# A tile per row for x, seven quarter products one chunk earlier, and a spread attention plan

## The chip, the cores and the metric

The kernel runs on one core of one Trainium2 chip. A core has five engines that run side by side, each through its own queue in order: TensorE (PE in the profile; its weight loads are PEld), VectorE (DVE), ScalarE (ACT), GpSimd (POOL) and SyncE (SP, which here only issues DMAs). Engines wait for each other through semaphores. Matmul results land in PSUM, eight banks of 512 fp32 columns on 128 partitions; the other engines carry them from there into SBUF. The metric is the device time of one execution in microseconds (us), the median over several runs.

## What is computed

Eight batch rows of causal attention with 8 heads, 576 positions and 64 features a head; four heads see a window of 32 positions, four a window of 128 with every fourth position. The rows' outputs, written one behind another as 4608 tokens of 512 features, go through a feed-forward layer with a squared ReLU:

```python
scores = scale * np.matmul(q, k.transpose(0, 1, 3, 2))        # (8, 8, 576, 576)
mask_plain = (rel >= 0) & (rel < 32)                            # heads 0..3
mask_dil = (rel >= 0) & (rel < 128) & (rel % 4 == 0)            # heads 4..7
attn = softmax(np.where(masks, scores, -1e9))
x = np.matmul(attn, v).transpose(0, 2, 1, 3).reshape(4608, 512)
r = np.maximum(x @ w_in, 0.0)                                   # w_in 512 x 2048
out = (r * r) @ w_out                                           # w_out 2048 x 512
```

## The kernel before

**Chunks and rows.** The tokens are cut into nine chunks of 512 (chunk 0 takes the 576 of row 0, chunk 1 only 448), and attention works by rows of 576. x, transposed, lies in one ring tile `xT` for three rows (lines 88 and 89); token t is column t mod 1728. Chunk c needs the end of one row and the start of the next. While TensorE multiplies chunk c, the attention of row c+1 is put between its matmuls.

**First product** (`mm1_gen`, L260 in `mm1_tile`): 16 slices of 128 hidden features, each 4 matmuls over the 512 inputs, into one of four PSUM banks used in turn. ScalarE does the ReLU into `rt` (L269), VectorE squares two slices at a time into `g` (L294). A slice gives two steps (`yield`), so a first product is 32 steps. A chunk that lies across the ring's end (chunks 3 and 6) is multiplied in two pieces, each with its own weight load.

**Second product.** Chunks 0 to 3 use `mm2_by_rows_gen` or `mm2_gen`: 64 matmuls of 512 columns (L301), 32 steps. Chunks 4 to 8 use `seven_gen`: quarter blocks of `g` and `w_out` and their sums, seven products of 16 matmuls of 256 columns each (L396), 28 steps. The sums of `g` (`S1`, `S2`, `S3`, lines 376 to 382) are made by VectorE behind the squares: `sums_behind` adds one behind the squares of steps 20 and 24, two behind those of 28 and 32. The sums of `w_out` (`T1` to `T4`, L365, eight subtractions) are made once, in chunk 2, every seventh step from step 4 on. VectorE also adds the seven products up (lines 450 to 491).

**Attention parts** (`row_parts`). s0, s1 (plain heads) and z0, z1 (dilated heads) make scores: matmuls into two PSUM pairs (L588, L602), two exps on ScalarE (L569), one product with the mask on VectorE (L573). They write `AT`, of which there is one. a0 to a2, d0, d1, e0, e1 multiply with v into one pair (L641, L655); VectorE normalizes them into `x_p` or `x_d` (L626, L627). x0, x1 and y0, y1 transpose the result into one pair (L670, L688), and ScalarE copies that into `xT` (L676, L694); x0 needs a0 and a1, x1 needs a1 and a2, y0 needs d0 and d1, y1 needs e0 and e1. From chunk 0's second product on the pairs are only two, used in turn, so each part waits for the one or two before it to be emptied. For rows 2 and 3 the transposes use a bank of the matmuls in place of a pair.

**The order** is written out by hand: a plan is a string of `step:part`, `run` sorts the parts by step and lets the matmul generator go on to each part's step before it. Each engine's queue follows from that order.

**Loading a row.** GpSimd issues the DMAs of q and k (L147, L223) and copies the plain heads into token order (`in_token_order`, L230); SyncE issues the transposing DMAs of the dilated heads (L248), stores of that copy (L236) and its transposing DMAs (L244), and the loads of v; GpSimd casts v (L202, L206). This goes one row ahead. For row 2 it stands in front of chunk 0's second product, whose plan is

```python
"4:t0 6:t1 8:s0:u0 10:s1:u1 12:z0 14:z1 18:a0 19:a1 20:a2 21:x0 22:d0 23:x1"
" 24:d1 25:e0 26:e1 27:y0 28:y1"
```

Of the kernel before, what the change touches and what calls it, by code (L numbers as in the profile page):

```python
# [8 lines left out]
FP16 = mybir.dt.float16  # L9
# [4 lines left out]
P = 128  # L14
# [3 lines left out]
def kernel(  # L18
# [9 lines left out]
    nc = tc.nc  # L28

    B, H, S, D = q.shape  # L30
    W = 32
    DIL = 4
# [4 lines left out]
    NDM = DM // P  # L37
# [18 lines left out]
    const = ctx.enter_context(tc.tile_pool(name="const", bufs=1))  # L56
# [18 lines left out]
    def bank(dt=FP32):  # L75
        i = turn["bank"] % 4
        turn["bank"] += 1
        b = PS[:, i, :]
        return b if dt == FP32 else b.bitcast(dt)
# [5 lines left out]
        return b if dt == FP32 else b.bitcast(dt)  # L85


    RING = 3 * S
    xT = const.tile([P, NDM, RING], FP16, name="xT")


    WI = ((0, 512), (512, 1024), (1024, 2048))
# [10 lines left out]
    def w_in_of(dmk, ffc):  # L103
        f = 512 * (ffc // 4) + ffc % 4
        t = 0 if f < 512 else 1 if f < 1024 else 2
        f -= WI[t][0]
        return wi[t][:, dmk, f : f + 509 : 4]
# [86 lines left out]
    def copy(eng, o, i):  # L194
        if eng is nc.scalar:
            nc.scalar.copy(o, i)
        else:
            eng.tensor_copy(o, i)
# [26 lines left out]
            )  # L225
        return d

    def in_token_order(b, n):
        o = natp.tile([P, 9, HH, D], FP16, name=f"o{b}", tag="o")
        nc.gpsimd.tensor_copy(o, n.rearrange("p h j d -> p j h d"))  # L230
        return o

    def keep_sliding_qk(b, o):
        d = dpool.tile([2, S, HH * D], FP16, name=f"dp{b}", tag="dp")
        for i in (1, 0):
            nc.sync.dma_start(  # L236
                out=d[i].rearrange("(p j) x -> p (j x)", j=9),
                in_=o[64 * i : 64 * (i + 1)].rearrange("p j h d -> p (j h d)"),
            )
        return d  # L240

    def transpose_sliding(b, dp):
        for i in (1, 0):
            nc.sync.dma_start_transpose(out=QKTp[b % 2][:, i, :, PADP:], in_=dp[i])  # L244

    def transpose_dilated(b, dd):
        for i in (1, 0):
            nc.sync.dma_start_transpose(out=QKTd[b % 2][:, i, :, KPAD:], in_=dd[i])  # L248
# [3 lines left out]
    def mm1_tile(ffc, t0, t1, rt):  # L252
        w = t1 - t0
        ph = bank()
        o = t0 % RING
        cut = min(w, RING - o)
        for dmk in range(NDM):
            for a, b, x in ((0, cut, o), (cut, w, 0)):
                if a < b:
                    nc.tensor.matmul(  # L260
                        ph[:, a:b],
                        w_in_of(dmk, ffc),
                        xT[:, dmk, x : x + b - a],
                        start=(dmk == 0 and a == 0),
                        stop=(dmk == NDM - 1 and b == w),
                    )
            if dmk == 1:
                yield
        nc.scalar.activation(rt, ph[:, 0:w], ACTF.Relu)  # L269
# [51 lines left out]
    def mm2_gen(c):  # L321
        for t in range(TOKC // P):
            po = bank()
            for ffc in range(NFF):
                mm2(c, po, t, ffc)
                if ffc % 2 == 1 and ffc < NFF - 1:
                    yield
            store(c, t, po)
            yield
# [165 lines left out]
    def moe_gen(c):  # L495
        yield from mm1_gen(c)
        yield from mm2_gen(c)

    def moe_seven_gen(c):
        yield from mm1_gen(c, sums_behind)  # L500
        yield from seven_gen(c)
# [162 lines left out]
    def x_sliding(b, half, xs, wide):  # L664
        px = pt(wide)
        for m3 in range(3):
            m = 3 * half + m3
            x = xs[m // 2][:, m % 2].rearrange("p h d -> p (h d)")
            for c in range(2):
                nc.tensor.transpose(  # L670
                    px[:, 288 * c + QB * m3 : 288 * c + QB * (m3 + 1)],
                    x[:, P * c : P * (c + 1)],
                    ident[0:QB, 0:QB],
                )
        t0 = (b % 3) * S + 288 * half
        nc.scalar.copy(  # L676
            xT[:, 0:2, t0 : t0 + 288],
            px[:, 0:UW].rearrange("x (c t) -> x c t", c=2),
        )

    def x_dilated(b, t, xs, wide):
        py = pt(wide)
        for a in range(2):
            for e in range(2):
                x = xs[a][:, e].rearrange("p h d -> p (h d)")
                for c in range(2):
                    o = 288 * c + QD * (2 * a + e)
                    nc.tensor.transpose(  # L688
                        py[:, o : o + QD],
                        x[0:QD, P * c : P * (c + 1)],  # L690
                        ident[0:QD, 0:QD],
                    )
        t0 = (b % 3) * S + 288 * t
        nc.scalar.copy(  # L694
            xT[:, 2:4, t0 : t0 + 288].rearrange("x c (i r) -> x c i r", r=DIL),
            py[:, 0:UW].rearrange("x (c r i) -> x c i r", c=2, r=DIL),
        )

    def row_parts(b, wide):

        xs, ys, zs = [], [], []
        return {
            "s0": lambda: s_sliding(b, 0),
            "s1": lambda: s_sliding(b, 1),
            "z0": lambda: s_dilated(b, 0),
            "z1": lambda: s_dilated(b, 1),
            "a0": lambda: xs.append(av_sliding(b, 0)),
            "a1": lambda: xs.append(av_sliding(b, 1)),
            "a2": lambda: xs.append(av_sliding(b, 2)),
            "x0": lambda: x_sliding(b, 0, xs, wide),  # L710
            "x1": lambda: x_sliding(b, 1, xs, wide),
            "d0": lambda: ys.append(av_dilated(b, 0, 0)),
            "d1": lambda: ys.append(av_dilated(b, 0, 1)),
            "e0": lambda: zs.append(av_dilated(b, 1, 0)),
            "e1": lambda: zs.append(av_dilated(b, 1, 1)),
            "y0": lambda: x_dilated(b, 0, ys, wide),
            "y1": lambda: x_dilated(b, 1, zs, wide),
        }

    def run(*plans, more=()):  # L720


        todo = list(more)
        for plan, parts in plans:
            for w in plan.split():
                step, *names = w.split(":")
                todo += [(int(step), parts[n]) for n in names]
        at = 0
        for step, part in sorted(todo, key=lambda t: t[0]):
            pump(step - at)  # L730
            at = max(at, step)
            part()
        pump(1000)
# [162 lines left out]
    n, dd = load_whole_sliding_qk(2), keep_dilated_qk(2)  # L896
    cast_sliding_v(1, 2)
    for t in range(2):
        for a in range(2):
            cast_dilated_v(1, t, a)  # L900
    o = in_token_order(2, n)
    transpose_dilated(2, dd)
    transpose_sliding(2, keep_sliding_qk(2, o))
    pending.append(mm2_by_rows_gen(0))
    parts = row_parts(1, True)
    parts.update(
        t0=lambda: t_sliding(1, ns1, 0),
        t1=lambda: t_sliding(1, ns1, 1),
# [5 lines left out]
            "4:t0 6:t1 8:s0:u0 10:s1:u1 12:z0 14:z1 18:a0 19:a1 20:a2 21:x0 22:d0 23:x1"  # L914
            " 24:d1 25:e0 26:e1 27:y0 28:y1",
            parts,
        )
    )
    load_v(2)

    rows_ = {b: row_parts(b, b > 3) for b in range(2, B)}
    SCORES = "{}:s0 {}:s1 {}:z0 {}:z1"
    VALUES = "{}:a0 {}:a1 {}:a2 {}:x0 {}:d0 {}:x1 {}:d1 {}:e0 {}:e1 {}:y0 {}:y1"
    for c in range(1, NTOKC):
        b = c + 1
        if b + 1 < B:
            see(QKTp[b % 2][0:1, 0, 0, PADP : PADP + 1])  # L930
            n, dd = load_whole_sliding_qk(b + 1), keep_dilated_qk(b + 1)
            o = in_token_order(b + 1, n)
            transpose_dilated(b + 1, dd)
            transpose_sliding(b + 1, keep_sliding_qk(b + 1, o))
        if b < B:
            cast_v(b)
        if b + 1 < B:
            load_v(b + 1)
        pending.append(moe_gen(c) if c < 4 else moe_seven_gen(c))
        plans, more = [], []  # L940
        if c < 3:
            plans.append((SCORES.format(*range(24, 40, 4)), rows_[b]))
            plans.append((VALUES.format(*range(40, 62, 2)), rows_[b]))
        if c == 2:
            it = sum_w_out_gen()
            more = [(4 + 7 * i, lambda it=it: next(it)) for i in range(8)]
        if c == 3:
            plans.append((SCORES.format(2, 8, 14, 20), rows_[b]))
            plans.append((VALUES.format(*range(24, 46, 2)), rows_[b]))
            plans.append((SCORES.format(47, 51, 55, 59), rows_[b + 1]))  # L950
        if 3 < c < B - 1:
            plans.append((VALUES.format(2, 5, 8, 11, 13, 16, 18, 22, 26, 29, 32), rows_[b]))
        if 3 < c < B - 2:
            plans.append((SCORES.format(36, 42, 48, 54), rows_[b + 1]))
        run(*plans, more=more)


# [28 lines left out]
```

## Time and profile before

| | |
|---|---|
| median of 3 runs | 311.64 us (311.43, 311.64, 315.43) |
| the profiled execution | 313.25 us, its span 311.2 us |
| granted TensorE clock | 1.00 throughout |
| matmul starts at chunk 0 | 20.0 us |
| DMA | 46.73 MB, mean 150 GB/s |
| L260, first product | 768 matmuls |
| L301, second product whole | 256 matmuls |
| L396, second product in seven | 560 matmuls |

The span runs from the first to the last instruction; the rest of the execution's time lies around it. A row of the timeline gives start, duration, engine, line, operation, what is written from what, the shape, how many instructions are merged, and in brackets the idle time before and what ended it. A matmul's duration holds the way through the array, so the distance between two starts is what it takes from the queue. The rows by stage give, for a window in us, the length of the window, then busy time and instructions of PE, PEld, DVE, ACT and POOL, the granted clock, the mean number for the DMA share, and GB/s.

By the starts of its first products the chunks begin at: c1 65.4, c2 96.1, c3 128.5, c4 163.3, c5 194.7, c6 226.3, c7 255.4, c8 281.4 us.

### The profile page before, as it was taken

The numbers are of one execution on the slowest core, as the hardware profiler recorded it, in microseconds if no ns is written. First come the engines' busy times: TensorE is split into PE (matmuls) and PEld (weight loads), VectorE is DVE, ScalarE is ACT, GpSimd is POOL, SyncE is SP. The second block draws the span as 40 slices with busy tenths as digits, with TensorE's granted clock in tenths as the row PEclk, the third lists the DMA queues.
The fourth block names the chain that finished last, engine by engine and source line by source line (L and its number), as shares of the span: only waits on it lengthen the run. The fifth ranks groups of instructions, "written<-read, shape, count | busy, mean of one in ns | idle before, by whom it ended". The sixth has DMA issues, their size and how long they took to land.

```text
span 311.2 us, 7133 instructions
## 1 busy us (share of the span) xinstructions
PE 297.2 (95%) x2932; PEld 200.7 (65%) x2932; DVE 198.2 (64%) x354; ACT 161.8 (52%) x286; POOL 85.4 (27%) x120
## 2 busy tenths in 40 slices
PE   3988999899999999999999999999999999999995
PEld 3657954455555555687545578657888885685584
DVE  6545645835852986297345879686868753863674
ACT  2646857278536772686356653565456406504610
POOL 5591027132703913283350344006000000000000
PEclk9999999999999999999999999999999999999999
DMA  7999989699979999998938894886120020012012
GB/s 117 242 205 212 213 185 234 156 227 206 224 180 220 266 196 164 248 235 166 236 134 185 162 216 122 190 173 141 67 71 3 2 101 34 2 46 91 0 36 101
DMA packets 75376, 46.73 MB, mean 150 GB/s; under 512 B 54416, under 2 KB 71056, under 8 KB 75152
## 3 DMA queue, kind: packets, MB, share of 16 engines
q1 hardware_dynamic: 67952, 32.52, 44.4%
q0 software_dynamic: 7248, 13.63, 24.7%
q8 instruction: 23, 0.38, 0.5%
q10 hardware_dynamic: 144, 0.13, 0.1%
q14 instruction: 9, 0.07, 0.1%
HBM read 39.85 MB, written 16.52 MB: 181 GB/s over the span
## 4 chain that ended last, share of the span: by engine, by line
PE 92%; DVE 2%; DMA 2%; ACT 2%; issue 1%; POOL 0%; DVEq 0%; POOLq 0%
PE PS L260 41%; PE PS L396 20%; PE PS L301 17%; PE PS L655 3%; PE PS L588 2%; PE PS L641 2%; PE PS L602 2%; DMA nd<-in_q_dram 2%; PE PS L688 1%; PE PS L670 1%; PE PS L523 1%; DVE AT L573 1%; ACT AT L569 1%; PE PS L581 1%; DVE x_p L627 1%
## 5 line engine op out<-in xcount | busy, mean ns | idle before, releaser
L260 PE MATMUL PS<-xT,wi 128*128 128x512 f16 (+6 forms) x768 | 136.1, 329 | 2.9 <-ACT xT L676 1.7
L269 ACT ACTIVATE rt<-PS 128x512 f16<-128x512 f32 (+2 forms) x160 | 88.7, 555 | 66.8 <-PE PS L260 64.0
L260 PEld LDWEIGHTS <-wi 128*128 128x128 f16 x768 | 79.2, 114 | 42.1 <-issue 3.0
L294 DVE TENSOR_TENSOR g<-rt 128x1024 f16<-128x1024 f16 (+1 forms) x64 | 47.6, 747 | 38.5 <-ACT rt L269 38.4
L301 PE MATMUL PS<-wo,g 128*128 128x512 f16 x256 | 64.4, 379 | 0.0
L569 ACT ACTIVATE AT<-PS 128x576 f16<-128x576 f32 x64 | 38.4, 650 | 19.8 <-PE PS L602 12.1
L396 PEld LDWEIGHTS <-S 128*128 128x128 f16 x320 | 31.0, 98 | 3.8
L301 PEld LDWEIGHTS <-g 128*128 128x128 f16 x256 | 21.3, 97 | 18.2
L396 PE MATMUL PS<-T,S 128*128 128x256 f16 x240 | 28.2, 273 | 0.0
L573 DVE TENSOR_TENSOR AT<-AT,maskp 128x1152 f16<-128x1152 f16 x14 | 15.0, 1072 | 19.1 <-ACT AT L569 19.1
L202 POOL CAST vp<-sv 128x512 f16<-128x512 f32 x24 | 20.6, 874 | 23.6 <-DMA sv<-in_v_dram 23.6
L206 POOL CAST vd<-sd 128x512 f16<-128x512 f32 x32 | 23.7, 773 | 10.5 <-DMA sd<-in_v_dram 10.4
L396 PEld LDWEIGHTS <-g 128*128 128x128 f16 x240 | 23.0, 98 | 3.2
L627 DVE TENSOR_TENSOR x_d<-PS,rcp_d 72x512 f16<-72x512 f32 x32 | 22.0, 687 | 1.1
L230 POOL COPY o<-n 128x2304 f16<-128x2304 f16 x6 | 13.0, 2172 | 30.6 <-issue 29.4
L396 PE MATMUL PS<-wo,g 128*128 128x256 f16 x160 | 19.5, 273 | 0.0
L676 ACT COPY xT<-PS 128x576 f16<-128x576 f16 x16 | 10.2, 637 | 14.6 <-PE PS L670 14.5
L573 DVE TENSOR_TENSOR AT<-AT,maskd 128x1152 f16<-128x1152 f16 x14 | 12.8, 917 | 7.3 <-ACT AT L569 7.3
L627 DVE TENSOR_TENSOR x_p<-PS,rcp_p 96x512 f16<-96x512 f32 x24 | 16.5, 687 | 0.8
L655 PEld LDWEIGHTS <-AT 128*128 128x128 f16 x256 | 12.4, 102 | 7.0 <-DVE x_d L627 1.3
L311 ACT COPY ot<-PS 128x512 f32<-128x512 f32 x16 | 9.4, 587 | 14.4 <-PE PS L301 14.4
L283 DVE TENSOR_TENSOR g<-rt 128x288 f16<-128x288 f16 x32 | 9.9, 309 | 9.9 <-ACT rt L269 9.8
(86 smaller groups left out, 257.3 us busy)
## 6 DMA issues: line engine op xcount, KB each, us to landing
sv<-in_v_dram SPq DMA_DIRECT2D x40, 128.0 KB, 4.0
out_dram<-c SPq DMA_DIRECT2D x19, 256.0 KB, 2.5
sd<-in_v_dram SPq DMA_DIRECT2D x8, 512.0 KB, 12.2
out_dram<-ot SPq DMA_DIRECT2D x15, 256.0 KB, 12.2
dp<-o SPq DMA_DIRECT2D x12, 288.0 KB, 3.8
sd<-in_v_dram SPq DMA_DIRECT2D x8, 288.0 KB
wo<-in_moe_w_out_dram POOLq DMA_DIRECT2D x4, 512.0 KB, 13.7
n<-in_k_dram POOLq DMA_DIRECT2D x6, 288.0 KB, 5.8
```

What stands on the lines that cost most here:

```text
L202: nc.gpsimd.tensor_copy(vp[b % 2][:, m : m + 2, :, 0:D], sv[:, m : m + 2, :, :])
L206: nc.gpsimd.tensor_copy(vd[b % 2][:, t, c : c + 2, :, 0:D], sd[:, t, :, D * c : D * (c + 2)].rearrange("p h (c d) -> p c h d", d=D),)
L230: nc.gpsimd.tensor_copy(o, n.rearrange("p h j d -> p j h d"))
L260: nc.tensor.matmul(ph[:, a:b], w_in_of(dmk, ffc), xT[:, dmk, x : x + b - a], start=(dmk == 0 and a == 0), stop=(dmk == NDM - 1 and b == w),)
L269: nc.scalar.activation(rt, ph[:, 0:w], ACTF.Relu)
L294: nc.vector.tensor_mul(g[:, f2 : f2 + 2, o:TOKC], rt[:, :, o:TOKC], rt[:, :, o:TOKC])
L301: nc.tensor.matmul(po, g[:, ffc, o + t * P : o + (t + 1) * P], w_out_of(ffc), start=(ffc == 0), stop=(ffc == NFF - 1),)
L396: nc.tensor.matmul(po[t], lhs(j)[:, t * P : (t + 1) * P], rhs(j), start=j == 0, stop=j == HF - 1)
L569: nc.scalar.activation(AT[:, u + i, 0:UW], ps[:, :, 0 : UW // 2], ACTF.Exp, scale=scale)
L573: nc.vector.tensor_mul(AT[:, u : u + n, 0:UW], AT[:, u : u + n, 0:UW], mask.unsqueeze(1).to_broadcast([P, n, UW]),)
L627: nc.vector.tensor_tensor(out=x[0:w], in0=pv[:, :, :, 0:D], in1=rcp[0:w].unsqueeze(3).to_broadcast([w, 2, HH, D]), op=ALU.mult,)
L655: nc.tensor.matmul(pav[:, e, h * (D + 2) : h * (D + 2) + D + 1], AT[:, 4 + 2 * a + t, off : off + P], vd[b % 2][:, t, 2 * a + e, h, 0 : D ...
```

## The change

x gets one tile a row in place of the ring, so every chunk that holds parts of two rows (2 to 7) is multiplied in two pieces. Chunk 3 uses the seven quarter products, and the sums of `w_out` are made at steps 4, 7, ... 25 of chunk 2. Plans are now a table by chunk: row 4's parts are spread over the whole of chunk 3, and of the next row's four score parts chunk 3 holds one, chunk 4 two and chunk 5 all four, where all three held all four; what is left over comes early in the following chunk. Row 2's copy into token order moves from GpSimd to ScalarE, and it and the DMAs that follow it are issued at step 17 of chunk 0's second product.

```diff
-    RING = 3 * S
-    xT = const.tile([P, NDM, RING], FP16, name="xT")
+    xT = [const.tile([P, NDM, S], FP16, name=f"xT{r}") for r in range(3)]
...
-    def in_token_order(b, n):
+    def in_token_order(b, n, eng=nc.gpsimd):
         o = natp.tile([P, 9, HH, D], FP16, name=f"o{b}", tag="o")
-        nc.gpsimd.tensor_copy(o, n.rearrange("p h j d -> p j h d"))
+        copy(eng, o, n.rearrange("p h j d -> p j h d"))
         return o
...
-        o = t0 % RING
-        cut = min(w, RING - o)
+        rows_in = [(r, max(t0, r * S), min(t1, (r + 1) * S)) for r in range(t0 // S, (t1 - 1) // S + 1)]
         for dmk in range(NDM):
-            for a, b, x in ((0, cut, o), (cut, w, 0)):
-                if a < b:
-                    nc.tensor.matmul(
-                        ph[:, a:b],
-                        w_in_of(dmk, ffc),
-                        xT[:, dmk, x : x + b - a],
-                        start=(dmk == 0 and a == 0),
-                        stop=(dmk == NDM - 1 and b == w),
-                    )
+            for r, a, b in rows_in:
+                nc.tensor.matmul(
+                    ph[:, a - t0 : b - t0],
+                    w_in_of(dmk, ffc),
+                    xT[r % 3][:, dmk, a - r * S : b - r * S],
+                    start=(dmk == 0 and a == t0),
+                    stop=(dmk == NDM - 1 and b == t1),
+                )
...
-    o = in_token_order(2, n)
-    transpose_dilated(2, dd)
-    transpose_sliding(2, keep_sliding_qk(2, o))
+
+    def turn_row_2():
+        transpose_dilated(2, dd)
+        transpose_sliding(2, keep_sliding_qk(2, in_token_order(2, n, nc.scalar)))
+
...
-        )
+        ),
+        more=[(17, turn_row_2)],
     )
     load_v(2)
...
+    SEVEN = 3
+    rows_ = {b: row_parts(b, b > SEVEN) for b in range(2, B)}
     SCORES = "{}:s0 {}:s1 {}:z0 {}:z1"
     VALUES = "{}:a0 {}:a1 {}:a2 {}:x0 {}:d0 {}:x1 {}:d1 {}:e0 {}:e1 {}:y0 {}:y1"
+    FAR = SCORES.format(*range(24, 40, 4)) + " " + VALUES.format(*range(40, 62, 2))
+    PLANS = {
+        1: (FAR, ""),
+        2: (FAR, ""),
+        3: (
+            SCORES.format(2, 8, 14, 20)
+            + " "
+            + VALUES.format(24, 27, 30, 33, 35, 38, 40, 44, 48, 51, 54),
+            "57:s0",
+        ),
+        4: (
+            "2:s1 7:z0 13:z1 " + VALUES.format(10, 15, 18, 21, 24, 27, 29, 33, 37, 40, 43),
+            "47:s0 53:s1",
+        ),
+        5: (
+            "2:z0 8:z1 " + VALUES.format(4, 7, 10, 13, 16, 18, 20, 24, 28, 31, 34),
+            SCORES.format(38, 43, 48, 53),
+        ),
+        6: (VALUES.format(2, 5, 8, 11, 13, 16, 18, 22, 26, 29, 32), ""),
+    }
...
-        pending.append(moe_gen(c) if c < 4 else moe_seven_gen(c))
-        plans, more = [], []
-        if c < 3:
-            plans.append((SCORES.format(*range(24, 40, 4)), rows_[b]))
-            plans.append((VALUES.format(*range(40, 62, 2)), rows_[b]))
-        if c == 2:
+        pending.append(moe_gen(c) if c < SEVEN else moe_seven_gen(c))
+        more = []
+        if c == SEVEN - 1:
             it = sum_w_out_gen()
-            more = [(4 + 7 * i, lambda it=it: next(it)) for i in range(8)]
-        if c == 3:
-            plans.append((SCORES.format(2, 8, 14, 20), rows_[b]))
-            plans.append((VALUES.format(*range(24, 46, 2)), rows_[b]))
-            plans.append((SCORES.format(47, 51, 55, 59), rows_[b + 1]))
-        if 3 < c < B - 1:
-            plans.append((VALUES.format(2, 5, 8, 11, 13, 16, 18, 22, 26, 29, 32), rows_[b]))
-        if 3 < c < B - 2:
-            plans.append((SCORES.format(36, 42, 48, 54), rows_[b + 1]))
-        run(*plans, more=more)
+            more = [(4 + 3 * i, lambda it=it: next(it)) for i in range(8)]
+        now, ahead = PLANS.get(c, ("", ""))
+        run((now, rows_.get(b)), (ahead, rows_.get(b + 1)), more=more)
```

In the copies L676 and L694 the target becomes `xT[b % 3]` with columns counted from the row's start.

More of the change, by code (lines that the diff above doesn't have):

```diff
@@ L674, in x_sliding @@
                 )
-        t0 = (b % 3) * S + 288 * half
+        t0 = 288 * half
         nc.scalar.copy(
-            xT[:, 0:2, t0 : t0 + 288],
+            xT[b % 3][:, 0:2, t0 : t0 + 288],
             px[:, 0:UW].rearrange("x (c t) -> x c t", c=2),
@@ L692, in x_dilated @@
                     )
-        t0 = (b % 3) * S + 288 * t
+        t0 = 288 * t
         nc.scalar.copy(
-            xT[:, 2:4, t0 : t0 + 288].rearrange("x c (i r) -> x c i r", r=DIL),
+            xT[b % 3][:, 2:4, t0 : t0 + 288].rearrange("x c (i r) -> x c i r", r=DIL),
             py[:, 0:UW].rearrange("x (c r i) -> x c i r", c=2, r=DIL),
@@ L916 @@
             parts,
-        )
+        ),
+        more=[(17, turn_row_2)],
     )
     load_v(2)
-    rows_ = {b: row_parts(b, b > 3) for b in range(2, B)}
+    SEVEN = 3
+    rows_ = {b: row_parts(b, b > SEVEN) for b in range(2, B)}
     SCORES = "{}:s0 {}:s1 {}:z0 {}:z1"
     VALUES = "{}:a0 {}:a1 {}:a2 {}:x0 {}:d0 {}:x1 {}:d1 {}:e0 {}:e1 {}:y0 {}:y1"
+    FAR = SCORES.format(*range(24, 40, 4)) + " " + VALUES.format(*range(40, 62, 2))
[18 more added lines that the diff above has]
+    }
     for c in range(1, NTOKC):
```

## The prediction

> **What bounds the kernel.** I read the page's busy shares and its chain first.
>
> ```profile
> PE 297.2 (95%) x2932; PEld 200.7 (65%) x2932; DVE 198.2 (64%) x354; ACT 161.8 (52%) x286; POOL 85.4 (27%) x120
> PE 92%; DVE 2%; DMA 2%; ACT 2%; issue 1%; POOL 0%; DVEq 0%; POOLq 0%
> ```
>
> TensorE is the bound. A part is worth what it takes from TensorE's queue, or from a wait in front of it. Next the sums by stage; c0 to c8 are the chunks.
>
> ```profile
> 146.00:163.42 17.42, 17.42 (x168) 8.59 (x166) 7.57 (x13) 8.59 (x15) 8.57 (x11) 1.00 0.76 184
> ...
> 180.74:194.85 14.11, 14.11 (x169) 11.79 (x168) 11.48 (x15) 6.16 (x11) 6.93 (x8) 1.00 0.71 163
> ...
> 243.31:255.54 12.23, 12.23 (x113) 10.93 (x112) 7.83 (x12) 1.48 (x3) 0.00 (x0) 1.00 0.13 46
> 255.54:269.35 13.81, 13.81 (x66) 7.29 (x65) 7.11 (x11) 8.96 (x15) 0.00 (x0) 1.00 0.11 37
> ```
>
> The first row is c3's second product (64 matmuls of 512 columns, plus attention), the second c4's with seven quarter products and four score parts, the third c6's with the seven alone, the last c7's first product: 64 matmuls of 512 columns, 0.2158 us each. So a step of the plans (two such matmuls) is 0.432 us, and a score part is (14.11 - 12.23) / 4 = 0.47.
>
> Then the waits on TensorE. From 66 us on, starts are a matmul's own time apart but for two waits of size. The timelines of c4 and c5 show them:
>
> ```profile
> 178.34 0.38 PE L260 MATMUL PS<-xT,wi 128*128 128x512 f16 x1
> 178.55 0.64 ACT L694 COPY xT<-PS 128x576 f16<-128x576 f16 x1
> ...
> 179.24 1.24 PE L260 MATMUL PS<-xT,wi 128*128 128x512 f16 x5 [0.51 <-ACT xT L694]
> ```
>
> ```profile
> 209.51 0.42 PE L688 MATMUL PS<-ident,x_d 72*128 72x72 f16 x8
> 210.66 0.59 PE L260 MATMUL PS<-xT,wi 128*128 128x512 f16 x2 [0.73 <-ACT xT L694]
> ```
>
> c4 multiplies rows 3 and 4 while that copy writes row 5's columns; c5 the like. They share only the one ring tile.
>
> In c0 a different wait, in its timeline:
>
> ```profile
> 53.62 2.11 POOL L230 COPY o<-n 128x2304 f16<-128x2304 f16 x1 [1.22 <-DMA n<-in_q_dram]
> ...
> 54.07 2.27 DVE L573 TENSOR_TENSOR AT<-AT,maskd 128x1152 f16<-128x1152 f16 x1 [0.94 <-ACT AT L569]
> ...
> 57.23 0.43 PE L641 MATMUL PS<-vp,AT 128*128 128x65 f16 x8 [1.09 <-DVE x_p L627]
> ```
>
> Beside GpSimd's copy the mask product takes 2.27 us; alone (52.36) it takes 0.76. The first x_p stands behind it, and the third value part waits for the PSUM pair that x_p empties.
>
> Last, the cost of short pieces, in c6, and of VectorE's sums, in c4:
>
> ```profile
> 227.20 0.42 PE L641 MATMUL PS<-vp,AT 128*128 128x65 f16 x8
> 227.46 1.47 PE L260 MATMUL PS<-xT,wi 128*128 128x384 f16 x12
> 228.77 0.42 PE L641 MATMUL PS<-vp,AT 128*128 128x65 f16 x8
> ```
>
> ```profile
> 178.60 0.68 DVE L294 TENSOR_TENSOR g<-rt 128x1024 f16<-128x1024 f16 x1
> 179.20 0.68 DVE L378 TENSOR_TENSOR S<-g 128x1024 f16<-128x1024 f16 x1
> 179.92 0.69 DVE L380 TENSOR_TENSOR S<-S,g 128x1024 f16<-128x1024 f16 x1
> ```
>
> Six pairs of 384 + 128 take 1.31 us, 0.2183 a pair: cutting costs 2.5 ns. Eight 65-column matmuls, each with its own weights, go every 0.0325 us (0.26 a part). A square and two sums hold VectorE for 2.0 us.
>
> **The change, part by part** (us of TensorE's time).
>
> *Seven products in c3:* 12.23 for 13.81, -1.58.
>
> *A tile per row:* in c4 the next matmul starts 0.90 after the one before, 0.68 late; in c5 209.51 + 0.26 = 209.77, so 0.89 late. A copy to another tile can hold no matmul: -1.57.
>
> *The price of the tiles:* today c3 and c6 are cut (at the ring's end); then every chunk from c2 to c7. c2, c4 and c5: 64 x 2.5 ns = 0.16 each, +0.48. c7 is cut 448 + 64, and no row has 64 columns on these weights. Between the pace of 65 columns (0.0325) and that of c6's 128-column piece (0.2183 - 0.1625 = 0.056) the pair is 0.1891 + 0.0325 to + 0.056, against 0.2158: +0.36 to +1.9. I take 0.36, since 65 columns is nearest. The same columns stream, so no gain is possible.
>
> The Trainium skill ("TensorE: Matmul & The Clock Gate", section "LDWEIGHTS (loading the stationary operand)") gives a load as its column count over 1.2 GHz, 107 ns for 128. By that rule, as an estimate, no piece could be shorter than 107 ns: the new cuts would cost about 10 us (3.4 in c2, 0.2 in c4, 1.7 in c5, 5.2 in c7) and the change would lose. c6 speaks against it: its 128-column pieces start the next matmul 56 ns later, weights included.
>
> *Row 2's copy on ScalarE.* ScalarE's relus take 543 ns for 448 columns and 598 for 512, 0.86 ns a column; from the 638 ns of a 576-column copy that makes 2.1 us for 2304. It stands behind the last exp (done 54.04; n landed by 53.62), so it runs until 56.2. Behind it in ScalarE's queue stand row 1's copies into xT, the first today at 58.51, at 57.3 then: 1 us to spare. At half the pace it would cost 1. On SyncE the moved transposes and stores pass nothing: chunk 0's output stores come from step 26 on, and o is wanted at 58.01, behind the dilated transposes. On GpSimd nothing follows until 66.7. VectorE's mask is then done at 54.8, the first x at 55.96 (value part 54.60 to 54.86, 0.17 to VectorE, 0.24 + 0.69); the third value part starts at 56.0 instead of 57.23: -1.2. The parts after it keep their distances.
>
> *w_out's sums every third step:* eight subtractions now at steps 4 to 25 of c2, where GpSimd's copy and casts (100.68 to 110.2) make VectorE's squares 1.09 long. By the queue the last square ends about 114.0 and the second product wants it at 113.9: +0.1 (0 to 1; nothing waited there before, so no gain).
>
> *The spread plans.* Score and value parts stay the same in number; their places change what stands in VectorE's queue. A part waits for a PSUM pair, and two pairs alternate; a value part's pair is free when VectorE has normalized it. c3 loses its waits of 0.15 and 0.16 in front of parts at 143.30 and 147.99: -0.3. New waits, walked through the queues with the durations above:
>
> - c5: z0 at step 2, a0 at 4, a1 at 7, z1 at 8. From c5's start: z0 0.86 to 1.33; ScalarE: relu 1.03, exps 1.54 and 2.09, done 2.74; a0 2.24 to 2.50; VectorE: mask 2.77, square 3.44, a0's reciprocal 4.04, its x done 4.97; a1 3.80 to 4.06, its x done 5.81. z1 would run at 4.49 and 4.72 and needs both pairs: its second half starts at 5.85, 1.1 late. Later e1 (28) stands behind a square and two sums, so y1 (34) comes 0.5 late. +1.6.
> - c4: a0's x (step 10) stands behind z0's mask and a square and is done 7.37 us into the chunk; z1 (13) wants the pair at 7.1: 0.3. d0's x (24) stands behind a square and a sum, done 16.1; d1 (29) wants its pair at 15.9: 0.2. e0's x (33) stands behind the last square and two sums, done 22.1; y0 (40) wants it at 21.7: 0.4. +0.9.
> - c3: its first product now has the sums too. By the clock of before: square 6 runs at 144.6, two sums until 146.6, a2's x (30) until 147.5; d0 (35) wants the pair at 146.7: +0.9.
>
> Each is 0 if the queue drains faster than this walk. Transposes landed for row 5 at 144.8 and row 6 at 175.8; their scores come later than that in both versions, so DMA stays hidden; were it not, every late microsecond would count whole.
>
> *Sum:* -1.58 - 1.57 - 1.2 - 0.3 = -4.65; +0.48 + 0.36 + 0.1 + 0.9 + 0.9 + 1.6 = +4.34. Net -0.3. The profiled run took 313.25 (span 311.2, 2.05 around it), 1.6 above the median of 311.64. The difference applied to the median gives 311.3.
>
> **Rivals.**
>
> *No new waits* (for: c4 and c5 of before run seven products, sums and values and waited for no pair; against: there value parts came before the sums of their step, and no score part came between). -4.65 + 0.94 = -3.7: 307.9.
>
> *GpSimd's copy lands on c4's sums: slower.* Row 7's copy starts 20 us after c3's end today (183.36 after 163.25). The new plan has c4's last sums at about 19.7 to 21.2. If the copy starts before the last sum has, VectorE is held 2 us as in c0, e0's pair with it, and y0 waits 2 longer: 313.3; with c5 slowed by the casts for row 7 (0.9) 314.2. Against: c3's last store, which row 6's transposes follow, comes later.
>
> *The ring is not the cause:* the two waits go on in c5, or show up as another wait on the copy: +0.9 to +1.6, 312.2 to 312.9. Against: c6, the same plan, does not wait, so it depends on columns.
>
> **How the numbers follow.** Forecast 0.5 (alone 309.8 to 312.6); no waits 0.22; copy on the sums 0.2; ring not the cause 0.08. The range takes in all four: 308.0 to 314.2. 2% (6.2 us, about what a measurement here tells from no change) lies outside all: even without any cost the gains stop at 4.65. Faster 0.03, within 0.93, slower 0.04.
>
> **What would show it.** c3's second product with no 512-column matmuls; no wait of L260 on L694 after 66 us; pieces of 128, 256, 320 columns in c2, c4, c5, and c7's first product 0.3 longer; no 2.27 us mask in c0 and the third value part 1.2 us earlier; in c5 z1's second half (L602) waiting about 1 us for x_p. If c5 shows no such wait, the walk is wrong and the time is near 308. If c7's first product grows by over 1 us, the 64-column price was wrong.

## The result, and the profile after

The changed kernel takes 314.44 us in the median of 20 runs (313.41 to 318.93), the kernel before 312.25 beside it (20 runs, 311.43 to 315.43). The ratio of the runs is 1.006, its 95% interval 1.0039 to 1.008: slower by about 1.9 us (the medians alone are 2.2 us apart), where 0.3 us less was forecast. The time lies just above the range; 0.6 of the 3.1 us between forecast and median is the kernel before, whose median is 312.25 over these runs and was 311.64 over three.

The profiled execution after took 313.48 us (span 311.5, before 311.2). Its page, engines and chain of waits:

```profile
PE 295.4 (95%) x3236; PEld 222.0 (71%) x3236; DVE 204.9 (66%) x369; ACT 162.2 (52%) x284; POOL 83.3 (27%) x119
...
PE 81%; DVE 8%; DMA 5%; ACT 2%; POOL 1%; issue 1%; POOLq 0%; ACTq 0%
```

TensorE is as busy as before, with 304 more and shorter matmuls. The chain is the news: VectorE's part of it went from 2% to 8%, which points to waits for VectorE. The windows by stage say where. Columns as before: window, its length, busy time and instructions of PE, PEld, DVE, ACT, POOL, clock, DMA share, GB/s; the rows are c3's second product, c4's second, c5's first and second, and c7's first:

```profile
143.79:159.54 15.75, 15.11 (x187) 13.04 (x185) 12.79 (x25) 4.93 (x8) 8.35 (x11) 1.00 0.82 190
177.43:192.01 14.58, 14.35 (x170) 12.37 (x168) 13.06 (x20) 4.84 (x8) 7.45 (x8) 1.00 0.67 163
192.01:210.91 18.90, 18.04 (x238) 15.62 (x237) 13.47 (x25) 12.54 (x22) 1.55 (x3) 1.00 0.86 186
210.91:226.29 15.38, 14.54 (x179) 12.09 (x178) 12.09 (x18) 6.89 (x12) 4.64 (x5) 1.00 0.20 62
255.34:269.54 14.20, 14.20 (x130) 9.39 (x128) 6.99 (x11) 8.96 (x15) 0.00 (x0) 1.00 0.11 38
```

In c5 TensorE is idle for 0.86 and 0.84 of these lengths; in c7 for nothing, there the short pieces themselves cost. Set out by the distance from the first matmul of a chunk to that of the next (us, worked out from the starts in the two traces):

| chunk | before | after | difference | predicted difference |
|---|---|---|---|---|
| c0, c1 | 76.09 | 74.57 | -1.52 | -1.2 |
| c2 | 32.37 | 32.61 | +0.24 | +0.26 |
| c3 | 34.79 | 32.42 | -2.37 | -2.39 |
| c4 | 31.43 | 32.48 | +1.05 | +0.85 |
| c5 | 31.64 | 34.27 | +2.63 | +1.81 |
| c6, c8 | 54.97 | 54.97 | 0 | 0 |
| c7 | 26.04 | 26.44 | +0.40 | +0.36 |

(The predicted differences are the terms of the sum put to their chunks, with 0.47 for each score part that the plans move: three out of c3, one into c4, two into c5.) From c2 on the changed kernel is 1.95 us longer, which is what the runs measure. The profile alone would have said otherwise: in its c0 and c1 this execution is 1.5 us ahead, and that is not there in the mean over executions, as the experiments show. Of the 1.52, 0.97 lies in c0's second product. The other 0.55 lies in its first, where the matmuls of 288 columns start every 0.222 us at first and every 0.123 us later: until 24.6 us in the profile before, until 21.8 in the one after. The profile after gives a granted clock of 0.50 for 19.4 to 22.7 us; the one before gives 1.00 there at the same slow pace, so "1.00 throughout" in the table of before does not describe its start.

In c0 the copy is now on ScalarE, and the second mask beside it takes 0.76:

```profile
53.51 2.11 ACT L195 COPY o<-n 128x2304 f16<-128x2304 f16 x1
53.65 0.76 DVE L570 TENSOR_TENSOR AT<-AT,maskd 128x1152 f16<-128x1152 f16 x1 [0.72 <-ACT AT L566]
...
55.63 0.36 PE L638 MATMUL PS<-vp,AT 128*128 128x65 f16 x6
```

The third value part (55.63) starts 15.55 us behind the start of c0's second product; before it was 16.53.

The two waits on L694 are gone. In their place, the timeline of c5's head:

```profile
195.91 0.42 PE L638 MATMUL PS<-vp,AT 128*128 128x65 f16 x8
...
197.10 0.30 PE L599 MATMUL PS<-QKTd 64*128 64x72 f16 x8 [0.33 <-DVE x_p L624]
...
197.19 0.69 DVE L624 TENSOR_TENSOR x_p<-PS,rcp_p 96x512 f16<-96x512 f32 x1
...
197.94 0.26 PE L599 MATMUL PS<-QKTd 64*128 64x72 f16 x5 [0.53 <-DVE x_p L624]
```

(Lines behind 254 are 3 lower than before: L599 is the dilated score matmul, L624 the normalizing product.) 197.10 and 197.94 are the two halves of z1. Each waits for VectorE to empty the pair of a value part; by the starts they are 0.50 and 0.70 late. The second stands 5.93 us behind c5's start at 192.01; the walk said 5.85. Later in the same chunk:

```profile
209.13 0.61 POOL L201 CAST vp<-sv 128x512 f16<-128x512 f32 x1 [1.69 <-PE PS L652]
209.52 0.77 DVE L291 TENSOR_TENSOR g<-rt 128x1024 f16<-128x1024 f16 x1
...
210.21 0.68 DVE L375 TENSOR_TENSOR S<-g 128x1024 f16<-128x1024 f16 x1
...
210.58 0.78 POOL L201 CAST vp<-sv 128x512 f16<-128x512 f32 x1 [0.84 <-DMA sv<-in_v_dram]
...
210.92 0.98 DVE L377 TENSOR_TENSOR S<-S,g 128x1024 f16<-128x1024 f16 x1
...
212.05 0.69 DVE L624 TENSOR_TENSOR x_d<-PS,rcp_d 72x512 f16<-72x512 f32 x1
...
212.79 0.42 PE L685 MATMUL PS<-ident,x_d 72*128 72x72 f16 x8 [0.84 <-DVE x_d L624]
```

e1's x_d (212.05) stands behind a square and two sums, and y1 (L685) comes 1.01 late by the starts; 0.5 had been put down for it.

### The profile page after: what moved, and what is told of

It is laid out like the page before. It is cut to its first block, busy times and chain, and to the rows that moved or that the text cites. A ratio compares the mean times of both kernels' runs of the same rounds, so it can differ in the third digit from the quotient of the medians.

```text
span 311.5 us, 7759 instructions
## 1 busy us (share of the span) xinstructions
PE 295.4 (95%) x3236; PEld 222.0 (71%) x3236; DVE 204.9 (66%) x369; ACT 162.2 (52%) x284; POOL 83.3 (27%) x119
## 4 chain that ended last, share of the span: by engine, by line
PE 81%; DVE 8%; DMA 5%; ACT 2%; POOL 1%; issue 1%; POOLq 0%; ACTq 0%
PE PS L257 36%; PE PS L393 22%; PE PS L298 13%; DMA wi<-in_moe_w_in_dram 2%; PE PS L652 2%; DMA sd<-in_v_dram 2%; DVE g L291 2%; DVE x_p L624 2%; PE PS L585 2%; PE PS L599 1%; PE PS L685 1%; PE PS L667 1%; PE PS L638 1%; DVE x_d L624 1%; ACT AT L566 1%
## 5 line engine op out<-in xcount | busy, mean ns | idle before, releaser
L257 PE MATMUL PS<-xT,wi 128*128 128x288 f16 (+8 forms) x1024 | 136.2, 288 | 1.8 <-DMA wi<-in_moe_w_in_dram 1.1
L257 PEld LDWEIGHTS <-wi 128*128 128x128 f16 x1024 | 97.2, 114 | 28.6 <-DMA wi<-in_moe_w_in_dram 1.3
L298 PE MATMUL PS<-wo,g 128*128 128x512 f16 x192 | 48.8, 379 | 0.0
L393 PEld LDWEIGHTS <-S 128*128 128x128 f16 x384 | 36.9, 98 | 4.5
L393 PE MATMUL PS<-T,S 128*128 128x256 f16 x288 | 34.6, 273 | 0.0
L205 POOL CAST vd<-sd 128x512 f16<-128x512 f32 x32 | 25.1, 818 | 7.9 <-DMA sd<-in_v_dram 7.7
L201 POOL CAST vp<-sv 128x512 f16<-128x512 f32 x24 | 18.7, 798 | 25.6 <-PE PS L257 17.8
L393 PE MATMUL PS<-wo,g 128*128 128x256 f16 x192 | 23.9, 273 | 0.0
L624 DVE TENSOR_TENSOR x_d<-PS,rcp_d 72x512 f16<-72x512 f32 x32 | 22.0, 687 | 1.1
L691 ACT COPY xT<-PS 128x576 f16<-128x576 f16 x16 | 10.2, 639 | 15.6 <-PE PS L685 15.4
L624 DVE TENSOR_TENSOR x_p<-PS,rcp_p 96x512 f16<-96x512 f32 x24 | 16.5, 687 | 0.8
L673 ACT COPY xT<-PS 128x576 f16<-128x576 f16 x16 | 10.2, 638 | 11.9 <-PE PS L667 11.4
L570 DVE TENSOR_TENSOR AT<-AT,maskd 128x1152 f16<-128x1152 f16 x14 | 11.0, 791 | 6.7 <-ACT AT L566 6.7
```

What stands on the lines that cost most here:

```text
L201: nc.gpsimd.tensor_copy(vp[b % 2][:, m : m + 2, :, 0:D], sv[:, m : m + 2, :, :])
L205: nc.gpsimd.tensor_copy(vd[b % 2][:, t, c : c + 2, :, 0:D], sd[:, t, :, D * c : D * (c + 2)].rearrange("p h (c d) -> p c h d", d=D),)
L257: nc.tensor.matmul(ph[:, a - t0 : b - t0], w_in_of(dmk, ffc), xT[r % 3][:, dmk, a - r * S : b - r * S], start=(dmk == 0 and a == t0), stop ...
L298: nc.tensor.matmul(po, g[:, ffc, o + t * P : o + (t + 1) * P], w_out_of(ffc), start=(ffc == 0), stop=(ffc == NFF - 1),)
L393: nc.tensor.matmul(po[t], lhs(j)[:, t * P : (t + 1) * P], rhs(j), start=j == 0, stop=j == HF - 1)
L570: nc.vector.tensor_mul(AT[:, u : u + n, 0:UW], AT[:, u : u + n, 0:UW], mask.unsqueeze(1).to_broadcast([P, n, UW]),)
```

## The experiments

"Ratio" is the time to that of the kernel before on the same chip, with the 95% interval. Stage lengths are distances between first matmuls, as above.

### Undoing the spread plans alone

The change with the plans of c3 to c5 as they were (tiles, seven products and row 2's copy kept):

```diff
-            + VALUES.format(24, 27, 30, 33, 35, 38, 40, 44, 48, 51, 54),
-            "57:s0",
+            SCORES.format(2, 8, 14, 20) + " " + VALUES.format(*range(24, 46, 2)),
+            SCORES.format(47, 51, 55, 59),
...
+        4: (VALUES.format(2, 5, 8, 11, 13, 16, 18, 22, 26, 29, 32), SCORES.format(36, 42, 48, 54)),
+        5: (VALUES.format(2, 5, 8, 11, 13, 16, 18, 22, 26, 29, 32), SCORES.format(36, 42, 48, 54)),
```

> The changed kernel with the plans of chunks 3 to 6 as they were before; the tiles, the seven products in chunk 3, the early sums of w_out and ScalarE's copy stay. Theory (value and score parts placed behind squares and sums in VectorE's queue keep PSUM pairs full): the waits of chunk 5 (0.50 and 0.70 before z1, 0.15, 1.01 before y0) and chunk 4 (0.32, 0.32, 0.39) go; chunk 4 and chunk 5 take about 30.9 us each by the starts of their products (32.5 and 34.3 in the changed kernel), chunk 3 33.4 to 34.2 for one score group too many; in all about 3 us under the changed kernel, ratio to before about 0.993. Rival (the 256 additional matmul pieces and weight loads, or the start, cost the time): chunks 4 and 5 still long, ratio 1.002 or more.

Ratio 1.0001 (0.9975 to 1.0027). c4 takes 30.96 and c5 30.92 without a wait of size, so the waits there are the plan's. But c3 takes 35.58 and not the 33.4 to 34.2 expected, with waits of 0.76, 1.32 and 0.62 for x_p and x_d: its sums and the old, dense value parts share VectorE. That is why the ratio is not the expected 0.993. The spread plan gains 3.2 us in c3 and pays 1.5 in c4 and 3.4 in c5; 1.4 of it on either side are the three score parts that only change their chunk.

### One part of the change at a time

Three kernels are the one before with one part: a tile per row; row 2's copy on ScalarE at step 17; seven products in chunk 3.

```diff
-        pending.append(moe_gen(c) if c < 4 else moe_seven_gen(c))
+        pending.append(moe_gen(c) if c < 3 else moe_seven_gen(c))
```

> The kernel before with a tile per row for x and nothing else. Theory: the two waits on the copy L694 in chunks 4 and 5 go (-0.68, -0.89), chunks 2, 4 and 5 get 0.16 each and chunk 7 0.40: net -0.7, ratio 0.997 to 0.999. Rival (pieces are the cost): the first products grow by more than 0.2 each where nothing waits, ratio above 1.002. If the copy was not the cause of the waits, another wait of the same size stands there and the ratio is about 1.003.

Ratio 0.9983 (0.9955 to 1.0012). c4's first product goes from 17.32 to 16.81 and c5's from 17.53 to 16.82, the waits on L694 gone: the shared tile was their cause, and that rival falls. The cuts cost +0.16 in c2 and +0.40 in c7. In the profiled execution c4's second product had a wait of 1.30: row 7's copy on GpSimd began 0.30 us before a sum of VectorE, which took 2.59 us, and TensorE waited for an addition behind it. The ratio's interval takes in both the expected gain and no change.

> The kernel before with row 2's copy in token order on ScalarE at step 17 and nothing else. Theory: the mask product in chunk 0 takes 0.76 in place of 2.27, chunk 0's second product is 1.0 shorter (24.74 to about 23.8), nothing after it changes: ratio 0.996 to 0.998. Rival (what is won in chunk 0 is lost again in chunk 1 or 2, since the loads of the next rows set their own pace): chunk 1 or 2 longer by as much, ratio 1.000.

Ratio 0.9993 (0.9962 to 1.0025): nothing gained. The timeline of c0 shows why:

```profile
52.97 2.81 POOL L206 CAST vd<-sd 128x512 f16<-128x512 f32 x4
53.20 2.11 DVE L573 TENSOR_TENSOR AT<-AT,maskd 128x1152 f16<-128x1152 f16 x1 [0.80 <-ACT AT L569]
...
55.64 2.11 ACT L196 COPY o<-n 128x2304 f16<-128x2304 f16 x1 [2.47 <-DMA n<-in_q_dram]
...
56.21 0.27 PE L641 MATMUL PS<-vp,AT 128*128 128x65 f16 x3 [0.94 <-DVE x_p L627]
```

The copy is on ScalarE, takes the predicted 2.1 us and begins 2.4 us after the mask does, when n has landed. The mask takes 2.11 us all the same, now beside GpSimd's casts of row 1's v, and the third value part waits as before. The copy was one of two neighbours that hold the mask; which of them lies there depends on when the loads land. In c1 of this execution, the value parts of row 2 find v not yet cast, for the casts stand in GpSimd's queue behind the copy of row 3:

```profile
80.65 2.10 POOL L198 COPY o<-n 128x2304 f16<-128x2304 f16 x1 [5.26 <-issue]
...
82.70 1.70 POOL L202 CAST vp<-sv 128x512 f16<-128x512 f32 x2
83.89 0.41 PE L641 MATMUL PS<-vp,AT 128*128 128x65 f16 x8 [1.83 <-POOL vp L202]
```

> The kernel before with seven quarter products from chunk 3 on and nothing else (its plans and the sums of w_out every seventh step stay). Theory: chunk 3's second product loses 1.58, and the sums of g now in chunk 3's first product hold VectorE 2.0 us at a time, so parts d0 or d1 behind them wait 0.5 to 1.2 for a pair: net -0.4 to -1.1, ratio 0.996 to 0.999. Rival (VectorE's additional 8 us in chunk 3 cost more than the product saves): chunk 3 not shorter, ratio 1.000 or more.

Ratio 1.0015 (0.9983 to 1.0047). c3 takes 36.72 in place of 34.79: the 1.58 us of fewer columns are more than given back by waits of 1.89, 1.33 and 0.62. Part of the 1.89 is this execution's (casts until 142.3 lengthen the squares and sums in front); the run that undid the plans has the same plan in c3, waits 0.76 there, and its c3 is still 0.79 longer than before. The ratio's interval takes in no change. With the old, dense plan seven products do not pay in c3.

### Row 2's copy: the change without it, and both kernels again

> The kernel before, profiled a second time. The prediction's reading of chunk 0 (GpSimd's copy holds the mask product, 1.2 us): chunk 0's second product takes 24.7 again. Rival (it depends on when row 2's DMA lands in that execution): it takes 23.5 to 24.7 with the copy at another place against the mask, and chunk 1 may wait for v of row 2 in exchange.

The profiled run took 313.16 us. This second execution of the kernel before has a wait of 1.10 us at the same value part (56.70), but GpSimd ran casts until 55.2 and the copy only from 55.26 on. The two masks in front, merged in the row at 51.99, began before the copy did and took 2.73 and 1.16 us:

```profile
51.99 3.81 DVE L573 TENSOR_TENSOR AT<-AT,maskd 128x1152 f16<-128x1152 f16 x2 [1.11 <-ACT AT L569]
...
52.38 2.81 POOL L206 CAST vd<-sd 128x512 f16<-128x512 f32 x4
...
55.26 2.52 POOL L230 COPY o<-n 128x2304 f16<-128x2304 f16 x1
...
56.70 0.43 PE L641 MATMUL PS<-vp,AT 128*128 128x65 f16 x8 [0.93 <-DVE x_p L627]
```

The wait that the prediction put down to the copy came with the casts in its place. That c0's second product took 24.91, as the prediction's reading would have it, is therefore no support for that reading.

> The changed kernel with row 2's copy on GpSimd and in its place before chunk 0's second product. The prediction's step (the copy on ScalarE is worth 1.2 us): ratio to before about 0.004 higher than the changed kernel's, 1.009 to 1.011. The theory after the first runs (chunks 0 and 1 follow the landing of row 2's q, k and v, and the copy's engine makes no lasting difference): the same as the changed kernel, 1.004 to 1.008.

```diff
...
+    o = in_token_order(2, n)
+    transpose_dilated(2, dd)
+    transpose_sliding(2, keep_sliding_qk(2, o))
...
-        more=[(17, turn_row_2)],
```

> The changed kernel again, beside the other three. From chunk 2 on as in its first profile (c3 32.4, c4 32.5, c5 34.3, c7 first 14.2); chunks 0 and 1 between 74 and 77 us by what row 2's DMAs do; ratio 1.004 to 1.008.

On one chip, the change with the copy back on GpSimd has ratio 1.0049 (1.0025 to 1.0072), the change itself 1.0048 (1.0019 to 1.0077). The copy's place is worth nothing that can be measured. The difference of these two ratios and the ratio of the copy alone are each known to about 1.2 us only, so that either by itself barely leaves out a gain of 1.2; the argument rests on the two together and on the profiles. Over all sixteen profiles, c2 begins at 95.4 us in the mean of the five with the copy on GpSimd (94.75 to 96.10) and at 95.2 in the eleven with it on ScalarE (94.09 to 97.14). On ScalarE the copy can cost as well: in the profile of the next experiment it began only at 55.05, row 1's copy into xT stood behind it until 57.06, and x1 in c0 waited 0.59. And c1 waits for the casts of v, 0.2 to 2.2 us, in seven of the sixteen profiles, with the copy on either engine.

### The waits in c4 and c5

c5's z1 in front of all value parts:

```diff
-            "2:z0 8:z1 " + VALUES.format(4, 7, 10, 13, 16, 18, 20, 24, 28, 31, 34),
+            "2:z0 6:z1 " + VALUES.format(8, 10, 12, 14, 16, 18, 20, 24, 28, 31, 34),
```

> The changed kernel with one plan string different: in chunk 5 z1 at step 6 in place of 8, a0, a1, a2 at 8, 10, 12 in place of 4, 7, 10, x0 at 14 in place of 13, the rest as it is. Theory (z1 needs both PSUM pairs right behind two value parts that VectorE has not normalized): the waits of 0.50 and 0.70 at the first z1 go, the wait of 1.0 before y1 stays, chunk 5's first product 18.90 to about 17.7; ratio to before 1.001 to 1.003. Rival (VectorE or ScalarE is full in chunk 5, the order does not matter): the first product stays above 18.5, the wait only stands before another part.

Ratio 1.0059 (1.003 to 1.0088). z1's wait is gone, but c5 takes 33.92 and not 34.27, 0.35 less for a wait of 1.20: a2 now waits 0.51, and y1 1.26. That is between the theory's 17.7 and the rival's 18.5 for c5's first product, which took 18.30. The place of the wait moved on in part: 0.51 now stands before a2, while 1.26 at y1 lies inside what executions of the changed plan gave there (1.01 to 1.70). So a part moved within VectorE's queue can hand its wait on; that the queue can hold all of c5's work in another order is shown by the last version below, where c5 takes 31.84.

c4 replanned as well (and c5 as in the last experiment, its last seven value parts one step earlier):

```diff
-            "2:s1 7:z0 13:z1 " + VALUES.format(10, 15, 18, 21, 24, 27, 29, 33, 37, 40, 43),
+            "2:s1 6:z0 10:z1 " + VALUES.format(13, 15, 18, 21, 23, 25, 27, 31, 35, 38, 41),
```

> The changed kernel with chunks 4 and 5 planned so that the score parts of a chunk come before its value parts and each of d0, d1, e0 and (in chunk 5) e1 stands one step in front of the squares and sums of steps 20, 24, 28 and 32 in place of behind them; the number of parts in each chunk is unchanged. Theory: no wait for a pair of over 0.2 in chunks 4 and 5; chunk 4 about 31.5 (32.5 in the changed kernel), chunk 5 about 31.9 (34.3): 3 us under the changed kernel, ratio to before 0.995 to 0.998. Rival (the waits come from the load of VectorE, not from the order): over 33 in chunk 5, ratio above 1.000.

Ratio 0.9988 (0.996 to 1.0016). c4 takes 31.60 (after 32.48) and c5 32.96 (34.27), in c5 with waits of 0.51 and 0.44 left, and so more than the 31.9 and the 0.995 to 0.998 that were expected. So 2.2 us of the loss were the places of the parts.

The change with the ring tile in place of the three tiles:

> The changed kernel with the ring in place of the tile per row. Theory: chunks 2, 4 and 5 lose the 0.16 of their pieces and chunk 7 the 0.40; in chunk 5 the first product gets back the wait on the copy L694 (y0 at step 31), 0.9, or part of it where other waits cover it; chunk 4 does not wait on it, since there y0 and y1 now come in the second product. If the ring was not the cause of the waits, no first product waits for L694.

The profiled run took 313.39 us (median of before there 312.08). c2's first product is 0.16 and c7's 0.40 shorter, but c5, 34.20, is no longer than with the tiles. The timeline shows the wait on L694 back, and what it hides:

```profile
211.62 0.59 PE L260 MATMUL PS<-xT,wi 128*128 128x512 f16 x2 [0.73 <-ACT xT L694]
...
213.09 0.42 PE L688 MATMUL PS<-ident,x_d 72*128 72x72 f16 x8
```

While TensorE waits 0.89 by the starts, VectorE catches up, and y1 (L688) waits 0.17 instead of 1.01. In c4 the new plan has y0 and y1 in the second product, where L260 no longer runs. By the stages of this one execution, the tiles gain nothing with this plan and cost their cuts; the ratio of this kernel was not measured.

The sums of `w_out` at every seventh step again:

```diff
-            more = [(4 + 3 * i, lambda it=it: next(it)) for i in range(8)]
+            more = [(4 + 7 * i, lambda it=it: next(it)) for i in range(8)]
```

> The changed kernel with the sums of w_out every seventh step, as before. Theory: the wait of chunk 2's second product for late squares (0.61, 0.41, 0.14 and 0.74 in four of the profiles with early sums, none in others) goes: 0 to 0.5 us under the changed kernel. The prediction had 0.1.

Ratio 1.003 (1.0005 to 1.0055) beside 1.0048 for the change on the same chip: the wait in c2's second product (0.26 us in the second execution of the change) is gone, too small for the intervals. In the seven profiles with the early sums this wait is between 0 and 0.74 us, 0.4 in the mean, where the prediction put 0.1.

### A version that beats both

Put together (the kernel called e9 in the expectations): seven products in c3, the ring, which saves the cuts, the sums at every seventh step, and parts placed by the queue of VectorE:

```diff
-            + VALUES.format(24, 27, 30, 33, 35, 38, 40, 44, 48, 51, 54),
+            + VALUES.format(23, 25, 27, 33, 35, 38, 41, 44, 48, 51, 54),
...
-            "2:s1 7:z0 13:z1 " + VALUES.format(10, 15, 18, 21, 24, 27, 29, 33, 37, 40, 43),
+            "2:s1 6:z0 10:z1 " + VALUES.format(13, 15, 18, 21, 23, 25, 27, 31, 35, 38, 41),
...
-            "2:z0 8:z1 " + VALUES.format(4, 7, 10, 13, 16, 18, 20, 24, 28, 31, 34),
-            SCORES.format(38, 43, 48, 53),
+            "2:z0 6:z1 " + VALUES.format(8, 10, 14, 15, 18, 19, 22, 25, 29, 34, 38),
+            SCORES.format(41, 46, 50, 54),
```

> The changed kernel with the ring in place of the tile per row, the sums of w_out every seventh step again, and plans in which a part of a pair comes no sooner than its pair can be normalized: chunk 3 has a0, a1, a2 at 23, 25, 27 and d1 at 41; chunk 4 as in the replanned run; chunk 5 z1 at 6, values at 8, 10, 14, 15, 18, 19, 22, 25, 29, 34, 38 and row 7's scores at 41, 46, 50, 54, so that y0 and y1 come in the second product, where no matmul reads xT. Theory: chunk 3 31.5 to 31.7, chunk 4 31.3 to 31.5, chunk 5 31.7 to 32.0, chunk 7's first product 13.81; from chunk 2 on 3 us under the kernel before: ratio 0.988 to 0.993. Rival (seven products in chunk 3 give VectorE too much work for any order): waits of over 1 us in all left in chunks 3 to 5, ratio 0.996 or more.

Ratio 0.9886 (0.9851 to 0.9921), 310.24 us beside 313.64. c3 31.63, c5 31.84; but c4's second product took 15.92, for in this execution row 7's copy landed on the sums:

```profile
178.84 2.18 POOL L198 COPY o<-n 128x2304 f16<-128x2304 f16 x1 [4.45 <-issue]
...
179.09 2.48 DVE L380 TENSOR_TENSOR S<-S,g 128x1024 f16<-128x1024 f16 x1
...
182.46 0.42 PE L688 MATMUL PS<-ident,x_d 72*128 72x72 f16 x8 [1.81 <-DVE x_d L627]
```

That is the mechanism and the size of the prediction's slower rival, in another kernel than the changed one: the sum begins 0.25 us behind the copy, is held for its length, and y0 waits 1.98 by the starts. Whether it is there each time was asked by the same kernel again, and by one with y0 and y1 of c4 at steps 43 and 45:

> The kernel of e9 again. If the wait before y0 in chunk 4 belongs to the plan: it is there again with 1.5 to 2 us, and the second product of chunk 4 takes 15.5 to 16. If it belongs to the execution: 14.1 to 15. The ratio in both cases 0.985 to 0.992.

Ratio 0.9887 (0.9843 to 0.9931). No such wait, and c4's second product takes 14.13:

```profile
179.39 0.69 DVE L380 TENSOR_TENSOR S<-S,g 128x1024 f16<-128x1024 f16 x1
...
179.77 2.28 POOL L198 COPY o<-n 128x2304 f16<-128x2304 f16 x1 [4.43 <-issue]
```

Here the copy came 0.38 us behind the same sum, which took its usual 0.69. The wait belongs to the execution.

> The kernel of e9 with chunk 4's y0 and y1 at the later steps 43 and 45 (38 and 41 in e9), row 6's scores behind them. If e9's wait of 1.98 us before y0 is GpSimd's copy of row 7 lying on the sums in front of the last x, and is there in every execution: the wait shrinks to under 0.5, chunk 4's second product goes from 15.92 to 14.1 to 14.6, and the ratio is 0.983 to 0.988. If the copy lands elsewhere each time: the wait is found at another place of chunks 4 and 5 or not at all, and the ratio stays within 0.004 of the repeated e9.

Ratio 0.9917 (0.9881 to 0.9953); c4's second product takes 13.94. In this execution the copy came 4.56 us behind that sum, so whether a later y0 would cover the wait stays open. c1 lost 1.33 us in it to the casts of v. From c2's first matmul to the last one the three profiles need 210.70, 208.51 and 208.32 us, the kernel before 211.24 and the changed one 213.19. The 2.7 us between before and the second execution account for most of the 3.5 us that 0.9887 makes of 312.89; what is left is inside the interval.

## Why the prediction was right and wrong

The step that failed is the gain of 1.2 us for row 2's copy; c5's waits, put down 0.76 too small, are the next in size.

- **Wrong: row 2's copy on ScalarE, "the third value part starts at 56.0 instead of 57.23: -1.2".** In the profile after something like it happened: the mask took 0.76 at 53.65, the third value part came 0.98 earlier within c0's second product, and that took 23.77 instead of 24.74. But it is no gain of the change: with the copy back the time is the same (1.0049 and 1.0048), alone it gives 0.9993. The step took one execution's collision for a fixture of the kernel. The copy starts when its load has landed or the casts in front of it are done (53.6 and 55.3 us in the two executions of before), casts held the mask in its place in two profiles, and in three of the five profiles with the copy on GpSimd c0's second product took 23.46 to 23.47, with no wait to remove.
- **Mis-sized: c5's new waits, "+1.6".** The walk named the right ones; they measure 2.36: z1 1.20 (1.1 predicted), y1 1.01 (0.5), and 0.15 at d1. y1 is the larger miss: the square and the second sum in front of it took 0.77 and 0.98 beside GpSimd's casts, where the walk used 0.68 and 0.69, so 0.38 of the missing 0.51 is this. Three other executions of the same places gave 1.05 to 1.70.
- **Right, within 0.2 us a chunk:** c3 (seven products, its plan, waits of 0.78 and 0.18 for the 0.9), c4 (0.32, 0.32 and 0.39 for 0.3, 0.2 and 0.4), c2, and c7. For c2 this is in part luck: in the profile after nothing waited for late squares, in the other six with the early sums something did.
- **The sum mended:** -0.3, +1.2 for the copy, +0.82 in c5, +0.20 in c4, +0.04 in the rest, makes +1.96; measured from c2 on +1.95, by the ratio +1.9. So close an agreement is luck, too: the wait at y1 alone is between 1.01 and 1.70 in four executions of the same places.
- **The tile per row, -1.57:** right against the old plan (c4 and c5 each lost their wait), but in the new plan it gains nothing in the one execution with the ring, since c4's parts have moved and c5's wait stands in for y1's. Taken one after the other the terms counted -0.89 for the tile in c5 and +0.5 for y1, which are one place in the queue.
- **64-column pieces:** c7's pair takes 14.20 / 64 = 0.222 us, 0.0328 for the piece beside 0.1891; of the two bounds the 65-column row was the right one. The rule that the prediction weighed (the Trainium skill, "TensorE: Matmul & The Clock Gate", "LDWEIGHTS (loading the stationary operand)", a load of 107 ns) is not what sets the pace here.
- **Rivals:** "No new waits" falls to the c5 timeline. "The ring is not the cause" falls to the tiles alone. The copy on c4's sums: in the profile after it came 1.36 us behind the last sum in front of y0 and lengthened only a later sum (1.72 us), for which nothing waited. It held y0 in one of the ten profiles with a spread c4, and it cost 1.30 at another place of c4 in the run with the tiles alone. How often it does is not settled; that it explains part of the spread of the runs was only argued.

## What to carry to other kernels

A collision of two engines seen in one execution is priced only after asking what its start hangs on: where that is a DMA's landing, look at a second execution before counting the gain. When a change adds work to an engine that evicts in order, walk that engine's queue as it will be, with durations taken beside the neighbour that will run, and count each stretch once, for one wait can stand in for another. Take the parts of a bundled change separately: here the seven products paid only together with the replanning, the tiles took away two waits under the old plan and under the new one a wait that another replaced, and the moved copy gained nothing that can be measured.

## What was not expected of the hardware

- A VectorE product of two SBUF operands can be held across several GpSimd instructions: masks took 2.11 us and 2.73 us beside casts back to back (0.76 alone). It is not always so: in the run that undid the plans a mask that began 0.19 us behind a cast took 1.03 us, and the next cast 1.13 instead of 0.61. What decides between the two is open. Products that read PSUM are not slowed: x_p and x_d took 0.69 beside casts and copies in every profile.
- Which of two starts first decides. The sum that began 0.25 us behind GpSimd's copy took 2.48 us; the same sum 0.38 us ahead of it took 0.69, and the copy 2.28 instead of 2.10. The Trainium skill ("SBUF — State Buffer", "Who interferes with whom") says that a VectorE instruction with two SBUF inputs contends with a GpSimd instruction that reads SBUF, and that issue order decides who blocks. This pair agrees, while the casts show that the wait can outlast one instruction.
